# A fused attention and MoE kernel: both first pairs loaded ahead of the branch, tile 0 first, and the x split set between a unit's slices

## The chip, the cores and the metric

The kernel runs on one core of a Trainium2 chip. The metric is the device time of one execution in microseconds (us); a kernel's time is the median of its runs. The core has five engines that run their own queues of instructions in order and meet at semaphores: PE (TensorE, matrix products into PSUM), DVE (VectorE), ACT (ScalarE), POOL (GpSimd) and SP (SyncE, which here issues all DMAs). PSUM is counted in banks; here three pairs of banks carry the tag `s`, and one bank each the tags `pv0` and `pv1`.

## The reference

Soft-capped attention over 4 batches of 12 heads, 448 tokens and 64 dimensions each, followed by a two-layer feed-forward with ELU, all in float32:

```python
scores = scale * np.matmul(q, k.transpose(0, 1, 3, 2))
scores = cap * np.tanh(scores / cap)
attn = np.exp(scores - max); attn = attn / (sum(attn) + 1e-09)
x = np.matmul(attn, v)            # to (1792 tokens, 768)
h = x @ w_in                      # (1792, 2048)
g = np.where(h > 0.0, h, np.exp(np.minimum(h, 0.0)) - 1.0)
out = g @ w_out                   # (1792, 768)
```

## The kernel before

**Branch.** `constants` loads the cap and derives a flag from it; with a cap up to 32 the fast path runs (no maximum is subtracted), else a general one that these inputs do not take. SP issues the loads of pair 0 (`pre`, keys and queries; then its values) ahead of the branch, all others behind it.

**Attention.** Two heads of a batch are a pair; 24 pairs, 6 to a batch. A pair's keys and queries come as one DMA of 448 KB: 64 columns with the first 64 keys, 448 with the queries, 384 with the other keys (`QK` = 896 columns). A round takes two pairs and has seven score tiles: tile 0 for the first 64 keys of both pairs (`tile0`, from the raw float32 tile), tiles 1 to 3 for the rest of the first pair and 4 to 6 for the second (`scores`, from a high and a low part that DVE makes: `prep_qk`, the cast `qkh` and the difference `qkl`, three products each). ACT takes tanh and then exp of each tile (`act`); PE multiplies p with the values (`values`, tile pv, in four steps t of which t = 0 is tile 0's), DVE adds p tiles (`add`, u) and PE sums them over keys (`sums`). DVE copies pv and sums out of PSUM (`take`: num and sums). The sums go by four small DMAs into den, DVE inverts them (`invert`), a DMA writes rec to DRAM, four DMAs spread it over partitions (`spread`, rb, two buffers), and DVE multiplies (`normalise`, x = num * rb).

**MoE.** x is split for float32-like products into xh (a cast) and xl (the rest): `Tokens.high` and `low`. The 16 slices of 128 hidden columns are taken two at a time (r) for each batch (b): a unit. `first` of a unit has, for each of its two slices, 18 matmuls of w_in into one bank (`hidden`) and an ELU (`elu`: exp on ACT (e), two DVE steps, cast gh on ACT, difference gl on DVE); `second` has 36 matmuls of w_out into three `s` tiles, which ACT or DVE adds up. Unit 0's two slices share one `s` tile (`begin`); the later ones have the tags pv0 and pv1. xh of batches 0 and 1 lies in memory of its own; that of batches 2 and 3 in the pool `late`, which takes over the memory that attention's tiles leave.

**Order.** In the fast path each engine runs its instructions in the order in which the program calls them. `Attention.run` collects calls with times in units of a tile (`AT` for a round's steps, `END` for the steps behind the last scores, where end = 84) and makes them sorted by time; `Moe.run` then loops over units in plain order. With `END`, unit 0 (b = 0) is put among the last round's steps: unit 0's first slice at 0.1, its second at 1.6, the ELUs at 1.76 and 3.0, `moe.first(0, 1)` at 4.0; the six splits of batch 1 from 0.2. A round's `take` of its last sums stands at end + 2.86, of its last num at end + 1.75. The raw tiles of pairs 1 and up rotate through two buffers; pair 0 is in `pre`, which later holds weights.

Of the kernel before, what the change touches and what calls it, by code (L numbers as in the profile page):

```python
# [7 lines left out]
F32 = mybir.dt.float32  # L8
# [8 lines left out]
B, H, S, D = 4, 12, 448, 64  # L17
P = 128
BANK = 512
NPAIR = B * H // 2  # L20
PPB = H // 2
# [15 lines left out]
K0 = D  # L37
QK = K0 + S + 3 * P
# [16 lines left out]
END = {  # L55
    "invert": 3.4, "spread": (3.8, 3.8), "normalise": (3.6, 4.2),
    "unit0": 0.1, "split": 0.2, "step": 0.1, "unit0b": 1.6, "elu0": 1.76, "elu1": 3.0, "unit1": 4.0,
}
# [125 lines left out]
class Moe:  # L184
# [42 lines left out]

    def first(self, r, b):
        for i in range(FT):
            t = self.ps.tile([P, BANK], F32, name=f"h{r * FT + i}_{b}", tag=f"pv{i}", bufs=1)  # L230
            h = t[:, :S]
            self.hidden(r, b, i, h)
            self.elu(r, b, i, h)

# [31 lines left out]
    def run(self):  # L266

        units = [(r, b) for r in range(NR) for b in range(B)]
        for i in range(1, len(units) + 1):
            if 1 < i < len(units):  # L270
                self.first(*units[i])
            for p in range((i + 1) * PPB, min((i + 2) * PPB, NPAIR)):
                self.x.split(p)
            self.wt.run(WSTEPS - 2)
            self.second(*units[i - 1])
            self.wt.run(2)
            self.wt.load()


class Attention:  # L280
# [51 lines left out]
    def tile0(self, n):  # L332


        s = self.room(n, 0)
        for i in range(2):
            raw = self.raw.pop(2 * n + i)
            for j in range(2):
                o, at = slice(j * D, j * D + D), (i ^ j) * D
                self.nc.tensor.matmul(  # L340
                    s[at : at + D, j, :S], raw[o, :K0], raw[o, K0 : K0 + S], start=True, stop=True
                )
# [96 lines left out]
    def run(self, weights, moe, raw, rawv):  # L439
        self.raw[0], self.v[0] = raw, rawv  # L440
        self.load(1)
        self.load_v(1)
        events = []

        def at(time, f, *a):
            events.append((time, len(events), f, a))

        rounds = NPAIR // 2
# [5 lines left out]
        for n in range(rounds):  # L454
            g = NG * n

            at(g + AT["tile0"] if n else 1.0, self.tile0, n)
            for time, groups in BURSTS.items():
                at(g + time if n or groups[0] > 1 else -1.0, self.scores, n, groups)
            for k in range(NG):  # L460
                at(g + k if n or k > 2 else (k - 1) % 3, self.act, n, k)
            for i in range(2):
# [8 lines left out]
                for f in ("spread", "normalise"):  # L471
                    at(min(g + AT[f][i], end + END[f][n // (rounds - 1)]), getattr(self, f), p)
                at(g + AT["load"][i], self.load, p + 4)
# [11 lines left out]
        for c in range(PPB):  # L485
            at(end + END["split"] + c * END["step"], self.x.split, PPB + c)
        h = []
# [4 lines left out]
        at(end + END["elu1"], lambda: moe.elu(0, 0, 1, h[1]))  # L492
        at(end + END["unit1"], moe.first, 0, 1)
        for _, _, f, a in sorted(events, key=lambda e: e[:2]):
# [79 lines left out]
def attention_elu_kernel(tc, qk, v, cap, w, out):  # L574
    nc = tc.nc
    src = (qk, v)
    with ExitStack() as outer:
# [7 lines left out]
        rawv0 = pre[:, QK : QK + NT * P].rearrange("p (t c) -> p t c", t=NT)  # L585
        nc.sync.dma_start(out=raw0, in_=qk[0])
        nc.sync.dma_start(out=rawv0, in_=v[0])
        fast = nc.values_load(flag[0:1, 0:1], min_val=0, max_val=1)

        def path(general):  # L590
            tag = "gf"[not general]
            with ExitStack() as ctx:
# [5 lines left out]
                with tc.tile_pool(name=f"at{tag}", bufs=1) as sb, tc.tile_pool(  # L598
                    name=f"dr{tag}", bufs=1, space=DRAM
                ) as dr:  # L600
                    if general:
# [6 lines left out]
                        for i, h in enumerate(moe.begin()):  # L608
                            moe.hidden(0, 0, i, h)
                            moe.elu(0, 0, i, h)  # L610
                        moe.first(0, 1)
                    else:
                        Attention(nc, sb, ps, dr, x, con, src, rawp).run(weights, moe, raw0, rawv0)
                with tc.tile_pool(name=f"late{tag}", bufs=1) as late:
# [53 lines left out]
```

## Time and profile before

| | us |
|---|---|
| median of three runs | 662.17 (654.52, 662.17, 662.73) |
| profiled execution, its own time | 653.14 |
| its span on the core | 651.0 |
| PE busy | 634.4 (97%) |
| DVE busy | 462.6 (71%) |
| ACT busy | 297.1 (46%) |
| POOL busy | 61.4 (9%) |

Times within the profile count from the span's start. The attention stage takes up to about 172 us, the rest is the MoE stage. A busy share is an average over both: ACT's 46% is nearly all in the first quarter. A matmul counts as busy until its modelled end, so the share of PE says little about its pace; the starts of two matmuls in a row tell it. A number in brackets behind a timeline's row is the idle time before it and what ended that.

### The profile page before, as it was taken

Reading aid. Unit: us, or ns where it says so; the run is one execution under the profiler, and the core shown is the slowest. Engines: PE = TensorE matmul, PEld = TensorE weight load, DVE = VectorE, ACT = ScalarE, POOL = GpSimd, SP = SyncE. Lnnn points to the kernel's source line nnn. Section 1 sums busy time; section 2 is a strip of 40 time slices with the busy share of each in tenths; the row PEclk is TensorE's granted clock in tenths of the full one; section 3 lists DMA queues with packets and bytes.
Section 4 is the critical chain, followed back from the end, with each engine's and each line's share of the span. In section 5 each row is a group of like instructions: output and inputs, shape, how many; then the busy total and the mean of one; then the engine's idle time right before and its main releaser. Section 6 shows DMA issues by size and latency. Waiting matters only on the chain.

```text
span 651.0 us, 8745 instructions
## 1 busy us (share of the span) xinstructions
PE 634.4 (97%) x3408; PEld 500.7 (77%) x3408; DVE 462.6 (71%) x672; ACT 297.1 (46%) x384; POOL 61.4 (9%) x40
## 2 busy tenths in 40 slices
PE   5999999999998999999999999999999999999996
PEld 2434344344487999999999999999999999999995
DVE  4789999999746766666667777666667777666443
ACT  5999999999725553222232222222232222222110
POOL 0010100100001111111111121111111111111000
PEclk9999999999999999999999999999999999999999
DMA  5445555543115021120202021020202021000224
GB/s 161 139 123 192 166 184 145 170 139 117 38 31 214 1 97 39 60 97 1 98 0 98 1 98 57 41 98 1 97 1 98 1 98 66 31 1 0 86 86 173
DMA packets 29776, 54.38 MB, mean 84 GB/s; under 512 B 13344, under 2 KB 19488, under 8 KB 29728
## 3 DMA queue, kind: packets, MB, share of 16 engines
q1 hardware_dynamic: 29728, 53.75, 24.2%
q8 instruction: 29, 0.48, 0.3%
q14 instruction: 19, 0.16, 0.1%
HBM read 47.97 MB, written 5.59 MB: 82 GB/s over the span
## 4 chain that ended last, share of the span: by engine, by line
PE 82%; DVE 10%; DMA 3%; issue 1%; ACT 1%; SPq 1%; POOL 0%; DVEq 0%; ACTq 0%
PE h L197 12%; PE h L196 12%; PE h L198 12%; PE o L197 11%; PE o L196 11%; PE o L198 11%; PE pv L365 7%; PE s L323 4%; DVE u L387 3%; DVE qkl L318 2%; PE sum L396 2%; DMA raw<-in_qk_dram 1%; DVE num L402 1%; DMA rb<-rec 1%; PE s L340 1%
## 5 line engine op out<-in xcount | busy, mean ns | idle before, releaser
L196 PE MATMUL h<-xh,wh 128*128 128x448 f32 x384 | 140.6, 366 | 2.0 <-ACT xh L174 1.9
L197 PE MATMUL h<-xl,wh 128*128 128x448 f32 x384 | 140.3, 365 | 0.2 <-DVE xl L180 0.2
L198 PE MATMUL h<-xh,wl 128*128 128x448 f32 x384 | 140.3, 365 | 0.0
L197 PE MATMUL o<-gl,wh 128*128 128x448 f32 x380 | 138.8, 365 | 0.0
L196 PE MATMUL o<-gh,wh 128*128 128x448 f32 x380 | 138.8, 365 | 0.0
L198 PE MATMUL o<-gh,wl 128*128 128x448 f32 x380 | 138.8, 365 | 0.0
L261 DVE TENSOR_TENSOR acc<-o,acc 128x896 f32<-128x896 f32 x83 | 85.9, 1083 | 9.4 <-PE o L198 9.4
L211 DVE TENSOR_SCALAR e<-e 128x448 f32<-128x448 f32 x64 | 25.2, 393 | 88.4 <-ACT e L210 88.3
L210 ACT ACTIVATE e<-h 128x448 f32<-128x448 f32 x64 | 34.8, 544 | 116.3 <-PE h L198 114.8
L358 ACT ACTIVATE p<-s,cap 128x896 f32<-128x896 f32 x84 | 84.8, 1009 | 2.7
L356 ACT ACTIVATE s<-s,tsc 128x896 f32<-128x896 f32 x84 | 81.9, 975 | 5.2 <-PE s L323 5.0
L365 PE MATMUL pv<-p,vf 128*64 128x448 f32 x368 | 79.3, 552 | 1.3 <-DVE num L402 1.2
L196 PEld LDWEIGHTS h<-xh,wh 128*128 128x128 f32 x384 | 72.1, 188 | 9.8 <-ACT xh L174 2.3
L197 PEld LDWEIGHTS h<-xl,wh 128*128 128x128 f32 x384 | 72.1, 188 | 6.3 <-DVE xl L180 0.5
L198 PEld LDWEIGHTS h<-xh,wl 128*128 128x128 f32 x384 | 72.1, 188 | 5.7
L196 PEld LDWEIGHTS o<-gh,wh 128*128 128x128 f32 x380 | 71.4, 188 | 5.7
L198 PEld LDWEIGHTS o<-gh,wl 128*128 128x128 f32 x380 | 71.4, 188 | 5.7
L197 PEld LDWEIGHTS o<-gl,wh 128*128 128x128 f32 x380 | 71.4, 188 | 5.7
L219 ACT ACTIVATE gh<-e 128x448 fp32r<-128x448 f32 x64 | 37.0, 578 | 75.7 <-DVE e L214 75.7
L220 DVE TENSOR_TENSOR gl<-e,gh 128x448 fp32r<-128x448 f32 x64 | 40.0, 625 | 41.3 <-ACT gh L219 41.3
L126 POOL TENSOR_TENSOR pre<-pre,wq 128x768 int32<-128x768 int32 x18 | 34.8, 1933 | 353.4 <-DVE pre L123 353.4
L365 PEld LDWEIGHTS pv<-p,vf 128*64 128x64 f32 x368 | 22.3, 136 | 42.3 <-issue 32.4
(70 smaller groups left out, 635.1 us busy)
## 6 DMA issues: line engine op xcount, KB each, us to landing
pre<-in_w_dram SPq DMA_DIRECT2D x18, 768.0 KB, 4.2
wr<-in_w_dram SPq DMA_DIRECT2D x14, 768.0 KB, 5.6
raw<-in_qk_dram SPq DMA_DIRECT2D x23, 448.0 KB, 4.4
vf<-in_v_dram SPq DMA_DIRECT2D x23, 256.0 KB, 4.2
rb<-rec SPq DMA_DIRECT2D x48, 112.0 KB, 2.8
out_dram<-acc SPq DMA_DIRECT2D x11, 448.0 KB, 2.6
den<-sums SPq DMA_DIRECT2D x96, 1.8 KB, 2.2
pre<-in_qk_dram SPq DMA_DIRECT2D x1, 448.0 KB, 4.0
```

The costliest lines, as they stand in the source:

```text
L126: nc.gpsimd.tensor_tensor(out=vi, in0=vi, in1=q, op=ALU.add)
L196: mm(acc, wh[:, m, :], ph, start=first, stop=False)
L197: mm(acc, wh[:, m, :], pl, start=False, stop=False)
L198: mm(acc, wl[:, m, :], ph, start=False, stop=last)
L210: nc.scalar.activation(out=ev, in_=h, func=AF.Exp)
L219: nc.scalar.activation(out=gh, in_=ev, func=AF.Copy)
L220: nc.vector.tensor_tensor(out=gl, in0=ev, in1=gh.bitcast(F32), op=ALU.subtract)
L261: self.nc.vector.tensor_tensor(out=o, in0=t, in1=o, op=ALU.add)
L323: yield lambda a=a, b=b, i=i: self.nc.tensor.matmul(s, a[o, k], b[o, :S], start=i == 0, stop=i == 2)
L356: self.nc.scalar.activation(out=s, in_=s, func=AF.Tanh, scale=self.con.tsc[:, 0:1])
L358: self.nc.scalar.activation(out=pt, in_=s, func=AF.Exp, scale=self.con.cap[:, 0:1])
L365: self.nc.tensor.matmul(out[o, :S], w[j], x[j], **flags)
```

## The change

It has three parts. (a) Pair 1 gets a tile of its own, `raw1`, and both pairs' keys and queries are loaded ahead of the branch, in two parts each: first the 512 columns that tile 0 reads, of pair 0 and pair 1, then the other 384 of each. Round 0 then follows the same table as the other rounds: tile 0 is its first group (ACT's too), where before it was third. (b) The times behind the last scores are new: unit 0's first ELU stands ahead of its second slice, the six xl of batch 1 behind the copy of the last sums, the last four x (`normalise`) ahead of unit 1. (c) `first` takes the list of pairs that are to be split behind the unit and sets three between its first ELU and its second slice and three before the second ELU; before, all six came behind both ELUs. Unit 1's `first` is called from `Moe.run`.

```diff
 END = {
-    "invert": 3.4, "spread": (3.8, 3.8), "normalise": (3.6, 4.2),
-    "unit0": 0.1, "split": 0.2, "step": 0.1, "unit0b": 1.6, "elu0": 1.76, "elu1": 3.0, "unit1": 4.0,
+    "invert": 2.95, "spread": 2.97, "normalise": 3.2, "unit0": 0.1, "xh": 0.2, "elu0": 1.55, "unit0b": 1.6,
+    "xl": 2.9, "elu1": 3.0,
 }
-    def first(self, r, b):
+    def first(self, r, b, behind=()):
+
+        behind = list(behind)
         for i in range(FT):
             t = self.ps.tile([P, BANK], F32, name=f"h{r * FT + i}_{b}", tag=f"pv{i}", bufs=1)
             h = t[:, :S]
             self.hidden(r, b, i, h)
-            self.elu(r, b, i, h)
+            if i == 0:
+                self.elu(r, b, i, h)
+            for p in behind[i * 3 : i * 3 + 3]:
+                self.x.split(p)
+            if i:
+                self.elu(r, b, i, h)
...
         for i in range(1, len(units) + 1):
-            if 1 < i < len(units):
-                self.first(*units[i])
-            for p in range((i + 1) * PPB, min((i + 2) * PPB, NPAIR)):
-                self.x.split(p)
+            if i < len(units):
+                self.first(*units[i], range((i + 1) * PPB, min((i + 2) * PPB, NPAIR)))
...
-            raw = self.raw.pop(2 * n + i)
+            raw = self.raw[2 * n + i]
...
-        self.raw[0], self.v[0] = raw, rawv
-        self.load(1)
+        self.raw.update(enumerate(raw))
+        self.v[0] = rawv
...
-            at(g + AT["tile0"] if n else 1.0, self.tile0, n)
+            at(g + AT["tile0"], self.tile0, n)
...
-                at(g + k if n or k > 2 else (k - 1) % 3, self.act, n, k)
+                at(g + k, self.act, n, k)
...
-                    at(min(g + AT[f][i], end + END[f][n // (rounds - 1)]), getattr(self, f), p)
+                    at(min(g + AT[f][i], end + END[f]), getattr(self, f), p)
...
-            at(end + END["split"] + c * END["step"], self.x.split, PPB + c)
+            at(end + END["xh"], self.x.high, PPB + c)
+            at(end + END["xl"], self.x.low, PPB + c)
...
-        at(end + END["unit1"], moe.first, 0, 1)
...
-        nc.sync.dma_start(out=raw0, in_=qk[0])
+        raw1 = cp.tile([P, QK], F32, name="raw1")
+
+        for c in (slice(0, K0 + S), slice(K0 + S, QK)):
+            for p, t in enumerate((raw0, raw1)):
+                nc.sync.dma_start(out=t[:, c], in_=qk[p][:, c])
         nc.sync.dma_start(out=rawv0, in_=v[0])
```

**At the start, PE.** These are PE's first instructions behind the branch, before the change (s0_1 is round 0's tile 1; `pre` is pair 0, raw1 pair 1):

```order
L323 MATMUL s0_1_125<-qkh0_119 128x448 x2
L323 MATMUL s0_1_125<-qkl0_120,qkh0_119 128x448 x2
L323 MATMUL s0_1_125<-qkh0_119,qkl0_120 128x448 x2
L323 MATMUL s0_2_132<-qkh0_119 128x448 x2
L323 MATMUL s0_2_132<-qkl0_120,qkh0_119 128x448 x2
L323 MATMUL s0_2_132<-qkh0_119,qkl0_120 128x448 x2
L340 MATMUL s0_0_146<-pre_84 64x448 x2
L340 MATMUL s0_0_146<-raw1_115 64x448 x2
```

and with it:

```order
L345 MATMUL s0_0_125<-pre_84 64x448 x2
L345 MATMUL s0_0_125<-raw1_85 64x448 x2
L328 MATMUL s0_1_132<-qkh0_121 128x448 x2
L328 MATMUL s0_1_132<-qkl0_122,qkh0_121 128x448 x2
L328 MATMUL s0_1_132<-qkh0_121,qkl0_122 128x448 x2
L328 MATMUL s0_2_139<-qkh0_121 128x448 x2
L328 MATMUL s0_2_139<-qkl0_122,qkh0_121 128x448 x2
L328 MATMUL s0_2_139<-qkh0_121,qkl0_122 128x448 x2
```

Tile 0 has moved from the third place to the first, ahead of the tiles that need DVE's cast; from tile 3 on the order is the same.

**At the start, SP.** SP's first DMAs behind the cap's, before the change (pre and raw0 to raw3 are pairs, vf their values; COMPARE_AND_BRANCH is the branch):

```order
L586 DMA pre_84<-in_qk_dram 128x896
L587 DMA pre_84<-in_v_dram 128x512
L588 TENSOR_LOAD flag_76
L588 ISA x2
L619 COMPARE_AND_BRANCH
L500 DMA raw1_115<-in_qk_dram 128x896
L507 DMA vf1_117<-in_v_dram 128x512
L500 DMA raw2_123<-in_qk_dram 128x896
L500 DMA raw3_154<-in_qk_dram 128x896
```

and with it:

```order
L594 DMA pre_84<-in_qk_dram 128x512
L594 DMA raw1_85<-in_qk_dram 128x512
L594 DMA pre_84<-in_qk_dram 128x384
L594 DMA raw1_85<-in_qk_dram 128x384
L595 DMA pre_84<-in_v_dram 128x512
L596 TENSOR_LOAD flag_76
...
L626 COMPARE_AND_BRANCH
L511 DMA vf1_119<-in_v_dram 128x512
L504 DMA raw2_130<-in_qk_dram 128x896
L504 DMA raw3_156<-in_qk_dram 128x896
```

Pair 1's keys and queries have moved ahead of the branch and, as pair 0's, come in two parts; pair 0's values are fifth where they were second, and raw2 and raw3 (pairs 2 and 3) are the first two in their tag.

**Behind the last scores, DVE.** From the last split of batch 1 on, before the change (num23 and sums23 are the last pair's copies out of PSUM, e0_0 and e1_0 the ELUs of unit 0's slices, den11 the last round's inversion):

```order
L180 TENSOR_TENSOR xl11_1971<-x11_1348,xh11_1969 128x448
L402 COPY num23_2000<-pv11_1_1909 128x448
L211 TENSOR_SCALAR e0_0_2002<-e0_0_2002 128x448
L214 SCALAR_TENSOR_TENSOR e0_0_2002<-h0_1922,e0_0_2002 128x448
L220 TENSOR_TENSOR gl0_0_2007<-e0_0_2002,gh0_0_2006 128x448
L405 COPY sums23_2016<-sum11_1_1977 128x448
L211 TENSOR_SCALAR e1_0_2022<-e1_0_2022 128x448
L214 SCALAR_TENSOR_TENSOR e1_0_2022<-h0_1922,e1_0_2022 128x448
L220 TENSOR_TENSOR gl1_0_2027<-e1_0_2022,gh1_0_2026 128x448
L417 SCALAR_TENSOR_TENSOR den11_1916<-den11_1916,eps_75 64x28
L420 RECIPROCAL den11_1916<-den11_1916 64x28
L437 TENSOR_TENSOR x20_2034<-num20_1764,rb20_2010 128x448
```

and with it, from unit 0's first ELU on, with five xl of the same form left out:

```order
L211 TENSOR_SCALAR e0_0_1972<-e0_0_1972 128x448
L214 SCALAR_TENSOR_TENSOR e0_0_1972<-h0_1924,e0_0_1972 128x448
L220 TENSOR_TENSOR gl0_0_1977<-e0_0_1972,gh0_0_1976 128x448
L407 COPY num23_1998<-pv11_1_1911 128x448
L410 COPY sums23_2006<-sum11_1_1967 128x448
L180 TENSOR_TENSOR xl6_2012<-x6_1031,xh6_1947 128x448
...
L422 SCALAR_TENSOR_TENSOR den11_1918<-den11_1918,eps_75 64x28
L425 RECIPROCAL den11_1918<-den11_1918 64x28
L211 TENSOR_SCALAR e1_0_2034<-e1_0_2034 128x448
L214 SCALAR_TENSOR_TENSOR e1_0_2034<-h0_1924,e1_0_2034 128x448
L220 TENSOR_TENSOR gl1_0_2039<-e1_0_2034,gh1_0_2038 128x448
L442 TENSOR_TENSOR x20_2042<-num20_1766,rb20_2000 128x448
```

The copies of num23 and sums23 have moved from behind six splits and around an ELU to directly behind that ELU; the splits stand behind them, and den11 ahead of the second ELU.

**Between unit 1's slices, DVE.** From the last x on, before the change (e0_1 and e1_1 are the ELUs of unit 1's slices, xl12 belongs to batch 2):

```order
L437 TENSOR_TENSOR x20_2034<-num20_1764,rb20_2010 128x448
L437 TENSOR_TENSOR x21_2036<-num21_1831,rb21_2013 128x448
L211 TENSOR_SCALAR e0_1_2063<-e0_1_2063 128x448
L214 SCALAR_TENSOR_TENSOR e0_1_2063<-h0_1_2044,e0_1_2063 128x448
L220 TENSOR_TENSOR gl0_1_2068<-e0_1_2063,gh0_1_2067 128x448
L211 TENSOR_SCALAR e1_1_2090<-e1_1_2090 128x448
L214 SCALAR_TENSOR_TENSOR e1_1_2090<-h1_1_2071,e1_1_2090 128x448
L220 TENSOR_TENSOR gl1_1_2095<-e1_1_2090,gh1_1_2094 128x448
L437 TENSOR_TENSOR x22_2098<-num22_1897,rb22_2038 128x448
L437 TENSOR_TENSOR x23_2100<-num23_2000,rb23_2041 128x448
L180 TENSOR_TENSOR xl12_2112<-x12_1504,xh12_2110 128x448
L180 TENSOR_TENSOR xl13_2116<-x13_1506,xh13_2114 128x448
```

and with it:

```order
L442 TENSOR_TENSOR x20_2042<-num20_1766,rb20_2000 128x448
L442 TENSOR_TENSOR x21_2044<-num21_1833,rb21_2003 128x448
L442 TENSOR_TENSOR x22_2046<-num22_1899,rb22_2028 128x448
L442 TENSOR_TENSOR x23_2048<-num23_1998,rb23_2031 128x448
L211 TENSOR_SCALAR e0_1_2077<-e0_1_2077 128x448
L214 SCALAR_TENSOR_TENSOR e0_1_2077<-h0_1_2058,e0_1_2077 128x448
L220 TENSOR_TENSOR gl0_1_2082<-e0_1_2077,gh0_1_2081 128x448
L180 TENSOR_TENSOR xl12_2087<-x12_1506,xh12_2085 128x448
L180 TENSOR_TENSOR xl13_2091<-x13_1508,xh13_2089 128x448
```

All four x stand ahead of unit 1's first ELU, and the splits of batch 2 behind that one ELU rather than behind both.

## Rows read from the trace of the kernel before

**Rows 1.** PE's waits, from 0 to 30 us, then 165 to 215: total us, times, longest.
```profile
PE s L323 <- DVE qkh L315: 6.0, 1, 6.0
...
PE h L196 <- ACT xh L174: 1.9, 1, 1.9
```

**Rows 2.** Timeline of the start: start us, us, engine, line, operation, out<-in, shapes, count.
```profile
1.21 0.42 SPq L586 DMA_DIRECT2D pre<-in_qk_dram  x1
1.67 0.43 SPq L587 DMA_DIRECT2D pre<-in_v_dram  x1
...
5.31 0.59 DVE L315 CAST qkh<-pre 128x832 fp32r<-128x832 f32 x1 [0.77 <-DMA pre<-in_qk_dram]
...
8.23 0.98 ACT L356 ACTIVATE s<-s,tsc 128x896 f32<-128x896 f32 x1 [3.88 <-PE s L323]
...
9.18 1.01 PE L340 MATMUL s<-pre 64*64 64x448 f32 x2
9.99 0.96 PE L340 MATMUL s<-raw 64*64 64x448 f32 x2
...
14.13 2.48 PE L365 MATMUL pv<-p,pre 128*64 128x448 f32 x12 [1.03 <-ACT p L358]
...
18.85 0.98 PE L340 MATMUL s<-raw 64*64 64x448 f32 x8
...
35.01 0.97 ACT L356 ACTIVATE s<-s,tsc 128x896 f32<-128x896 f32 x1
```

**Rows 3.** DMA issues of the first 12 us: kind, count, KB each, us from issue to landing.
```profile
pre<-in_qk_dram SPq DMA_DIRECT2D x1, 448.0 KB, 4.0
pre<-in_v_dram SPq DMA_DIRECT2D x1, 256.0 KB, 4.2
```

**Rows 4.** Busy us by windows: two rounds, then MoE stage; PE, PEld, DVE, ACT, POOL.
```profile
62.45:76.00 13.55, 13.55 (x94) 5.61 (x92) 13.17 (x20) 13.27 (x15) 0.75 (x1) 1.00 0.47 144
117.04:130.61 13.57, 13.57 (x94) 5.61 (x92) 13.50 (x21) 13.32 (x15) 0.00 (x0) 1.00 0.60 200
...
230.00:640.00 410.00, 410.00 (x2025) 379.92 (x2024) 272.07 (x378) 108.76 (x168) 48.14 (x26) 1.00 0.15 56
```

**Rows 5.** Timeline of the turn from attention to MoE, columns as in rows 2.
```profile
172.24 0.47 PE L196 MATMUL h<-xh,wh 128*128 128x448 f32 x1
173.81 2.69 DVE L180 TENSOR_TENSOR xl<-x,xh 128x448 fp32r<-128x448 f32 x5
...
178.62 0.47 PE L196 MATMUL h<-xh,wh 128*128 128x448 f32 x1
...
182.57 0.55 ACT L210 ACTIVATE e<-h 128x448 f32<-128x448 f32 x1 [7.52 <-PE h L198]
183.66 0.62 DVE L214 SCALAR_TENSOR_TENSOR e<-h,e 128x448 f32<-128x448 f32 x1
185.47 0.62 DVE L405 COPY sums<-sum 128x448 f32<-128x448 f32 x1
185.82 0.37 PE L198 MATMUL h<-xh,wl 128*128 128x448 f32 x1
186.23 0.44 PE L196 MATMUL h<-xh,wh 128*128 128x448 f32 x1
...
189.92 0.24 DVE L417 SCALAR_TENSOR_TENSOR den<-den,eps 64x28 f32<-64x28 f32 x1 [1.44 <-DMA den<-sums]
...
192.89 3.11 SPq L432 DMA_DIRECT2D rb<-rec  x4
...
197.26 0.37 PE L198 MATMUL o<-gh,wl 128*128 128x448 f32 x1
...
198.20 0.63 DVE L437 TENSOR_TENSOR x<-num,rb 128x448 f32<-128x448 f32 x1 [0.54 <-DMA rb<-rec]
198.91 2.92 ACT L174 ACTIVATE xh<-x 128x448 fp32r<-128x448 f32 x6 [3.59 <-DVE x L437]
...
200.51 0.36 PE L198 MATMUL h<-xh,wl 128*128 128x448 f32 x1
```

More of the change, by code (lines that the diff above doesn't have):

```diff
@@ L610, in path @@
                             moe.elu(0, 0, i, h)
-                        moe.first(0, 1)
                     else:
-                        Attention(nc, sb, ps, dr, x, con, src, rawp).run(weights, moe, raw0, rawv0)
+                        Attention(nc, sb, ps, dr, x, con, src, rawp).run(weights, moe, (raw0, raw1), rawv0)
                 with tc.tile_pool(name=f"late{tag}", bufs=1) as late:
```

## The prediction

> **What bounds the kernel now.** I read the page's engine rows first, then TensorE's waits by stretch, then the timelines of the two stretches in which those waits lie, and last the windows of the stretch between them. TensorE (PE) waits long at two places only: 6.0 us at the start, and 1.9 us at the first matmul of unit 2 [rows 1]; behind 215 us the view of its waits is empty. So 436 of the 651 us can change only by being started earlier, and the question is how much earlier.
>
> At the start ACT's first tanh stands at 8.23 [rows 2]. From there a tile's tanh and exp take 1.913 us (14 pitches from 8.23 to 35.01), 13.39 for a round of seven. But rounds take longer: one of 13.55 in which PE is busy all 13.55, a later one of 13.57 in which DVE is busy 13.50 [rows 4]. PE and DVE, and not ACT alone, carry the attention stage; a lead has to reach them.
>
> At the turn to the MoE stage, PE's last matmul of unit 0 starts at 197.26; at its pitch of 0.2025 (410 us for 2025 matmuls [rows 4]) the third matmul of unit 2 would start at 197.87, and it starts at 200.51 [rows 5]: 2.64 us lost. The chain behind it reads backwards: xh12 (198.91) waits for x23 (198.20), the last reader of the memory that xh12 takes over; x23 for the reciprocals' broadcast (rb, issued from 192.89, when their trip through rec in DRAM was over), that for den (189.92), that for the copy of the sums at 185.47. The copy could have run when the sums were there, ahead of 178.62, but stands in DVE's queue behind the ELU of unit 0's first slice, and that ELU started at 182.57, when the second slice was done.
>
> **The start, step by step.** Both pairs' keys and queries for tile 0 are 512 columns, 256 KB each, and now go first. In the trace 448 KB issued at 1.21 landed 4.0 later, at 5.21, and 256 KB more issued at 1.67 landed at 5.87 [rows 2, 3]. The new second transfer, issued at about 1.67, completes 512 KB: bounds 5.2 and 5.9, I take 5.5, as 512 KB lies near the first. Tile 0 starts at 5.6, takes 1.77 as it did at 9.18 (to 10.95), and ACT starts at 7.45: 0.8 earlier.
>
> The Trainium skill, "DMA: Bandwidth & Descriptors", section Bandwidth, speaks against the two parts: its table has 1 MB moved at 341 GB/s and 64 KB at 138. Worked out from that table (an estimate), 512 KB in small pieces would need up to 3.7 us of transfer instead of 1.5, ACT would start behind 8.23, and the sum below would be 2.4. No row here has transfers of 192 KB; the trace's one of 256 KB landed 4.2 after its issue, hardly behind the 4.0 of 448 KB.
>
> Tile 1 needs pair 0's second part, the third transfer (issued about 2.13, landed 6.1 to 6.4). From the cast to ACT's start was 2.92 (5.31 to 8.23), so it is ready at about 9.2, and ACT wants it at 9.36. That is in time by little; each 0.1 more costs 0.1.
>
> The larger gain is on PE. Before, the twelve value matmuls at 14.13 could not begin until the third exp, since the group's first operand (tile 0's p) was third on ACT. Now p0 and p1 are there and eight of the twelve run ahead of the third exp. Scores of tile 4 start when the second exp frees a bank, 7.45 + 3.83 = 11.3; 0.8 for six matmuls; then the 4.72 that PE took from 14.13 to 18.85 puts the next round's tile 0 at 16.8, where it must wait for the fifth exp, 7.45 + 9.57 = 17.0. Against 18.85 that is **1.8 us earlier**. The freeing of the raw buffers, and with it the load and casts of pairs 4 and 5 on SP and DVE, hangs on that same tile 0 and shifts too; pair 3's load no longer waits for pair 1's buffer. Since PE and DVE set the rounds, I carry 1.8 to the end of the stage. Bounds: 0.8 (ACT's lead alone), 2.2 (first parts there at 5.2).
>
> The early matmuls are slow: tile 0's eight took 1.77 at 9.18 and 0.98 at 18.85, though the page's clock row reads full in every slice. I priced tile 0 at 1.77 and the value matmuls at full pace, as at 14.13. The Trainium skill, "TensorE: Matmul & The Clock Gate", Part 1, says that "the default state is throttled, and activity releases the throttle"; the trace agrees. By that rule the pauses that the new order leaves PE (waiting for banks until 11.3) could bring the faster level later; its time is that of the second rival.
>
> **The turn, on the old clock (all of it shifts by 1.8).** PE's order is the same. The first slice starts at 172.24; the second took 3.95 from 178.62 to ACT's e at 182.57, so e for the first can start at 176.2. **A new wait:** both slices share one tile, so PE's second slice waits until DVE's second ELU step has read the first. That step ended 1.71 after e (183.66 + 0.62): 177.9, and PE has sums and values until 178.62. Covered by 0.7; queued behind it would be all of PE. From e to the copy of the sums was 2.90; now num23's copy (0.55) stands between: sums at 179.6 instead of 185.5. The six xl of unit 1, moved behind it, run at 0.54 each (five in 2.69 at 173.81) from 180.2; PE wants the first at 182.6, then one per 0.61. Hidden, by 1.8; without that cover each us would be one of PE.
>
> Then den, 4.45 behind the sums: 184.1; rb could go out 2.97 behind that (189.92 to 192.89), at 187.0. Now one detour: the ELU of slice 1 stands ahead of x20 and x21 on DVE, and rb22 takes rb20's buffer; x20 is done at about 187.4 (den's two steps to 184.6, 2.3 for the ELU, 0.5), so SP issues rb22 at 187.45. From there to x23's end 5.94 (192.89 to 198.83): 193.4. Behind it in DVE's queue stand unit 1's first ELU, then xl12 to xl17. The ELU holds DVE 2.35 (the 2.90 less e's 0.55), to 195.75, while ACT, behind gh, makes xh12 (0.5); xl12 is done at 196.4. PE needs it at 197.46: **margin 1.1 us, and the 2.64 go.** Also the copy of the sums held PE from 186.02 to 186.23 (second bank); that 0.2 goes. The den, rec and rb DMAs and the weights behind them on SP start some 5.5 earlier and have an idle queue. Slice 1's ELU of unit 1 comes behind xl17, its second step done at about 200.2; PE takes that bank at 200.9. In unit 2 the x split moves likewise and PE keeps a us. The xh and xl themselves are as many as before, under PE's matmuls.
>
> **Sum:** 1.8 + 2.64 + 0.2 = 4.6. The profiled span 651.0 becomes 646.4, its own time 653.14 (2.14 outside the span) 648.5. The three timed runs are 654.52, 662.17 and 662.73; the median lies 9.03 above the profiled execution, and nothing in this trace shows those 9 us. I take the same 4.6 off the median: **657.6**. If most of the new runs fall beside the profiled one, they read 648.5 to 650.
>
> **Rivals.** (1) The parts move side by side instead of one after another, and the first ones land with the last of the 896 KB: 5.87 for 704 KB and 0.66 for each 256 KB more give 6.4. ACT starts 0.9 later than reckoned, 3.7 are saved: 658.5. Against it: 448 KB landed 0.66 ahead of 704. The skill's table on small pieces, above, points the same way. (2) The head start is swallowed: tile 1 or PE's faster level comes late, ACT keeps 0 to 0.8 of its lead, and little but the turn is won: 2.8 to 3.6 saved, 659.0. For it: a margin of 0.1 at tile 1. Against it: PE waited 1.03 for ACT at 14.13, room that the new order fills. The skill's rule on the clock, above, is one way to it. (3) The turn's stall is kept, because unit 0's first e or DVE's queue is later than reckoned by over 1.1 + 2.6: 1.8 saved, 660.4. Against it: every link above has its own row. (4) The other side: x22 and x23 now stand ahead of unit 1's first ELU in DVE's queue, and while they wait for rb nothing behind them runs, xl12 included. Beyond 194.5 for x23's end each us costs PE one; at 199.1, behind even the old 198.83, all 4.6 are gone. At 200.1 the time is 663.2. Against it: from rb22's issue to x23 it would take 12.6 us instead of 5.9. (5) The edits change nothing that a run shows, the spread of the runs being larger: 662.
>
> **How the numbers follow.** Forecast 0.55, (1) 0.10, (2) 0.15, (3) 0.09, (4) 0.03, (5) 0.08. In all of them some two in five of the chance is for runs near the profiled execution rather than the median's level. The range runs from 647.5 (profiled level, with the upper bounds 2.2 + 2.8 saved 648.1, and half a us for what lies outside the span) to 661.5 (median's level, only 0.7 saved); the forecast's own range, given the median's level, is 656.6 to 659. Two per cent, about what a measurement of this kernel tells from no change, is 13 us, and no part here comes near it; faster by that only if the new median falls to the profiled level and all 4.6 come: 0.12. Slower by that: 0.03.
>
> **What would show it.** ACT's first tanh at 7.3 to 7.6; its second 1.91 later, with no wait for PE. Round 1's tile 0 near 17.0. The first matmul of unit 0 (172.24) near 170.4. In the waits of PE behind that: no xh or xl, and the second slice of unit 0 at no wait for DVE. The copy of the last sums 7.4 us, not 13.2, behind unit 0's first matmul. I am wrong if the rounds lengthen to give the 1.8 back, or if a PE wait on DVE appears at the second slice, at xl12 or at unit 2's second slice.

## The result, and the profile after

The changed kernel takes **648.26 us** (four executions, 648.10 to 648.50), the kernel before 658.94 beside it (654.52, 655.72, 662.17, 662.73). The ratio on record, 0.9886 with an interval of 0.9838 to 0.9935, is of fast executions, those within 1.5% of a kernel's fastest, and not that of the two medians; here the taller ones are part of what a kernel does, so the text gives all of them. The profiled execution of after has a span of 646.2 and a time of 648.27; forecast for it were 646.4 and 648.5. The forecast median, 657.6, was not met: all new executions lie at the profiled level. From profiled to profiled execution the gain is 4.87 us (653.14 to 648.27), between the medians 10.68. The other 5.8 us are the real finding.

TensorE's waits in the trace of after: total us, times, longest.

```profile
PE s L345 <- DMA pre<-in_qk_dram: 5.0, 1, 5.0
PE pv L370 <- DVE num L407: 1.7, 5, 0.7
PE s L328 <- DVE qkl L323: 0.3, 1, 0.3
```

The 1.9 us of [rows 1] are gone, and so is every wait behind 165 us. The first line names the DMA, but that part landed at 4.61 (below), 0.4 ahead of PE's start; most other runs with the new start have the same wait, of 5.1 to 5.3 us, for `DVE eps`, a step of the constants ahead of the branch. The start, columns as in [rows 2]:

```profile
5.02 1.01 PE L345 MATMUL s<-pre 64*64 64x448 f32 x2 [5.02 <-DMA pre<-in_qk_dram]
...
5.36 1.01 PE L345 MATMUL s<-raw 64*64 64x448 f32 x2
...
7.25 0.98 ACT L361 ACTIVATE s<-s,tsc 128x896 f32<-128x896 f32 x1 [2.88 <-PE s L345]
...
8.14 0.74 PE L328 MATMUL s<-qkl,qkh 64*128 64x448 f32 x2 [0.32 <-DVE qkl L323]
...
9.32 0.98 ACT L361 ACTIVATE s<-s,tsc 128x896 f32<-128x896 f32 x1
...
12.36 2.48 PE L370 MATMUL pv<-p,pre 128*64 128x448 f32 x12
...
17.14 0.98 PE L345 MATMUL s<-raw 64*64 64x448 f32 x8
```

And the DMA issues of the first 12 us, us from issue to landing, against [rows 3]:

```profile
pre<-in_qk_dram SPq DMA_DIRECT2D x1, 256.0 KB, 3.4
raw<-in_qk_dram SPq DMA_DIRECT2D x1, 256.0 KB, 3.6
...
pre<-in_qk_dram SPq DMA_DIRECT2D x1, 192.0 KB, 4.2
```

The second first part, issued at 1.67, is there at 5.27, and ACT starts 0.98 earlier than in [rows 2]. Its second tanh comes 2.07 behind the first, not 1.913: tile 1, for whose low halves PE waited 0.3, was 0.16 late. PE's tile 0 of round 1 stands 1.71 earlier (17.14 for 18.85).

The turn, against [rows 5]:

```profile
171.10 0.47 PE L196 MATMUL h<-xh,wh 128*128 128x448 f32 x1
...
175.04 0.55 ACT L210 ACTIVATE e<-h 128x448 f32<-128x448 f32 x1 [1.12 <-PE h L198]
...
178.39 0.61 DVE L410 COPY sums<-sum 128x448 f32<-128x448 f32 x1
...
178.93 3.29 DVE L180 TENSOR_TENSOR xl<-x,xh 128x448 fp32r<-128x448 f32 x6
...
182.84 0.24 DVE L422 SCALAR_TENSOR_TENSOR den<-den,eps 64x28 f32<-64x28 f32 x1 [0.62 <-DMA den<-sums]
...
186.29 2.37 SPq L437 DMA_DIRECT2D rb<-rec  x4
...
191.14 0.62 DVE L442 TENSOR_TENSOR x<-num,rb 128x448 f32<-128x448 f32 x1 [0.69 <-DMA rb<-rec]
...
193.25 2.90 ACT L174 ACTIVATE xh<-x 128x448 fp32r<-128x448 f32 x6
...
195.83 0.36 PE L196 MATMUL h<-xh,wh 128*128 128x448 f32 x1
```

xh12 is made from 193.25, and PE reaches unit 2 at 195.83 without stopping. **The gain by terms:** unit 0's first matmul is 1.14 earlier (172.24 to 171.10). The first output matmul behind unit 2's `first` (207.40 before, 203.12 after) is 4.28 earlier, so the turn gave 3.14. From there to the last matmuls nothing changes; what follows them was 0.5 us shorter. 1.14 + 3.14 + 0.5 = 4.8, the spans' difference. Two of these terms hold for this pair of traces only. Behind the last matmul come 5.1 to 5.7 us in the traces of this case, whatever the order, so the 0.5 is not the change's. And unit 0's first matmul stands at 171.84 and 171.89 in the two other traces with the old start, and at 170.86 to 171.15 in seven with the new one: the start is worth 1.0 there on average.

### The profile page after: what moved, and what is told of

Its sections match the earlier page's. It is cut to its first block, busy times and chain, and to the rows that moved or that the text cites. A ratio compares the mean times of both kernels' runs of the same rounds, so it can differ in the third digit from the quotient of the medians.

```text
span 646.2 us, 8747 instructions
## 1 busy us (share of the span) xinstructions
PE 633.9 (98%) x3408; PEld 501.8 (78%) x3408; DVE 462.5 (72%) x672; ACT 296.8 (46%) x384; POOL 61.4 (10%) x40
## 4 chain that ended last, share of the span: by engine, by line
PE 86%; DVE 9%; DMA 2%; issue 1%; SPq 0%; POOL 0%; DVEq 0%
PE h L196 12%; PE h L198 12%; PE h L197 12%; PE o L198 12%; PE o L197 12%; PE o L196 12%; PE pv L370 7%; PE s L328 5%; DVE u L392 3%; DVE qkl L323 2%; PE sum L401 2%; DVE num L407 1%; PE s L345 1%; DMA pre<-in_qk_dram 1%; DVE qkh L320 1%
```

## Experiments: which part, and what are the heights?

**The kernel before, again.** No edit.

> The kernel before, unchanged, to see span and time of each of its executions. All theories expect executions at two levels, near 654 and near 662 us. Theory A (what lies between the two levels has nothing to do with the edits): executions at 662 have a span of 651 and 11 us around it, or a longer span whose extra time lies anywhere. Theory B (the pause of TensorE at the turn makes the upper level): the extra 8 us lie in the span, behind 197 us, with matmuls at a wider pitch than 0.2025. Theory C (the start makes it): the extra 8 us lie in the span, ahead of round 1's tile 0, which then stands later than 18.85.

Its twelve executions and 74 more of the kernel before beside the other experiments have spans at four heights: 650.6 to 651.6 at a mean granted clock of 0.999 (11 of them; the profiled execution of before, 651.0, is such a one), 651.6 to 653.4 at 0.996 or 0.997 (41), 653.3 to 654.4 at 0.993 to 0.995 (10), and 660.4 to 663.7 (24, middle 661.1). Nothing lies between 657 and 662 us of time. So theory A in the form "outside the span" falls.

**The start alone.** The kernel before with the four first loads and `at(g + AT["tile0"], self.tile0, n)`, `at(g + k, self.act, n, k)`.

> The kernel before with the new start alone (both first pairs ahead of the branch in two parts, tile 0 first). All theories: ACT's first tanh at 7.25, unit 0's first matmul near 171.1 instead of 172.24, the wait of 1.9 us at unit 2's first matmul still there, since the chain of sums, den, rec, rb and x moves with it; span 651.0 - 1.1 = 649.9, or 649.4 if the last 0.5 us of the gain lie in the tail. Theory A and B: its executions still show two levels, about 652 and 660. Theory C: all of them lie within 0.5 us near 652.

Ratio 0.9989 (0.9947 to 1.0031). Two executions at full clock have 650.1, which is 0.9 under the middle of before's; but five of twelve stand at 659.8 to 660.7, and one of these is the profiled one, so that its trace shows the upper height. Its wait at unit 2, windows of it (us, then busy us and count of PE, PEld, DVE, ACT, POOL, then PEclk, DMA share, GB/s; PEld are PE's weight loads, PEclk the granted clock), and PE at a shorter pause, 11 us earlier:

```profile
PE h L196 <- ACT xh L174: 2.7, 1, 2.7
```

```profile
197.00:199.10 2.10, 0.00 (x0) 0.00 (x0) 0.63 (x1) 0.58 (x2) 0.00 (x0) 1.00 1.00 375
199.10:200.30 1.20, 0.97 (x2) 0.68 (x3) 1.17 (x3) 1.20 (x3) 0.00 (x0) 0.76 1.01 420
200.30:201.60 1.30, 1.30 (x5) 1.13 (x5) 1.30 (x3) 1.30 (x4) 0.00 (x0) 0.50 0.34 142
...
230.00:640.00 410.00, 410.00 (x1986) 372.41 (x1985) 266.98 (x371) 107.55 (x166) 48.03 (x26) 1.00 0.15 53
```

```profile
184.61 0.37 PE L198 MATMUL h<-xh,wl 128*128 128x448 f32 x1
185.02 0.44 PE L196 MATMUL h<-xh,wh 128*128 128x448 f32 x1
185.30 0.37 PE L197 MATMUL h<-xl,wh 128*128 128x448 f32 x1
```

The pause costs three times. First itself, 2.7 us. Second, behind it the granted clock is 0.50, the level of 1.2 GHz: for some 2.6 us the matmuls follow each other at 0.372 instead of 0.203, which costs 1.0 to 1.5. In the profiled execution of before the pause was 1.9 and the clock stayed full; in the one profiled here without an edit (span 652.0) it was 2.3, and the clock fell: that is the step from 651 to 652. No execution at 653.3 to 654.4 was profiled; that these lost more by the clock is read from their means alone. (The Trainium skill, "TensorE: Matmul & The Clock Gate", Part 1, has it that activity releases the throttle; this trace agrees as far as the 0.50 behind a pause goes.) Third, **the stream behind the pause runs at a wider pitch to the end of the kernel**: 1986 matmuls in 410 us where [rows 4] have 2025, at a clock that reads 1.00. From start to start that is 0.2067 for 0.2027 (the counts take in two at the edges of the window). Over the 2,200 matmuls left this is 8.8 us: the step to 661. It does not lie at the start, so theory C falls. But it does not begin at the long pause either: in this trace the matmuls go at 0.2067 from 185.30 on, behind the 0.2 us for which PE waits for the copy of the last sums, and the long pause leaves the pitch as it was. In the profiled executions of before at 651.0 and 652.0 the same short pause has 0.2067 behind it too, and the long one ends it. So this run alone does not say which of the two pauses makes the upper height.

**The turn alone.** The kernel after with the start of before.

> The kernel before with the new turn alone (first ELU ahead of the second slice, xl behind the sums, x split between a unit's slices). All theories: first tanh at 8.23, unit 0's first matmul at 172.24, no wait for xh or xl in unit 2; 2.64 for the stall, 0.2 for the bank and 0.3 for the wider pitch there are saved: span 651.0 - 3.1 = 647.9, or 647.4 with 0.5 in the tail. Theory A and C: its executions still show two levels, about 650 and 658. Theory B: all of them lie within 0.5 us near 650.

649.24 (649.20 to 649.50, six executions), ratio 0.9892 (0.9836 to 0.9949), spans 647.3 to 647.6, no wait of PE behind 165 us. The heights are gone with the two pauses: theory B. With the changed kernel and three of the runs below that have no pause there either (whole pairs, and the weight steps moved, all or two) it is 28 executions, all with spans of 645.9 to 647.9. The turn is worth 3.65 against before's executions at full clock (651.0), the start another 1.0 on top of it (649.24 to 648.26).

**Whole pairs instead of parts.** `for p, t in enumerate((raw0, raw1)): nc.sync.dma_start(out=t, in_=qk[p])`

> The changed kernel with the two first pairs loaded whole, in two DMAs of 448 KB, instead of four parts. Theory of the prediction (the transfers are served one after another, so the parts bring pair 1's keys and queries of tile 0 forward): pair 0 lands at about 5.2, pair 1 at about 6.4, tile 0's second half follows it, ACT's first tanh at 7.9 to 8.2 instead of 7.25, round 1's tile 0 0.4 to 0.8 later than 17.14, and 0.2 to 0.6 of it left in the span (646.4 to 646.8). Rival (the parts are served side by side, or the lead is lost later in the rounds whatever its size): the span stays at 646.2 within 0.1.

649.20 (648.95 to 649.65), ratio 0.9891 (0.9835 to 0.9948), span 647.1. Timeline:

```profile
6.38 1.76 PE L345 MATMUL s<-raw 64*64 64x448 f32 x4
...
8.26 0.98 ACT L361 ACTIVATE s<-s,tsc 128x896 f32<-128x896 f32 x1 [3.79 <-PE s L345]
```

Pair 1 lands at 6.37 when it is whole, and ACT starts a microsecond later. The parts are served one after another, as the prediction had it, and they are worth 0.9, a little more than expected. Preloading without parts would have left ACT at its old 8.23. It also has the time of the turn alone (649.20 and 649.24): with whole pairs the early load and tile 0's new place gain nothing that the time shows. Tile 0 of round 1 does come 0.9 earlier than in [rows 2], at 17.98, but unit 0's first matmul stands at 171.68, 0.2 ahead of the nearest trace with the old start. Tile 0's place was not tried without the early load.

**One short pause put back.** In the changed kernel DVE reads the sums' bank once more, behind the second ELU step of unit 0's second slice:

```
+        if hold is not None:
+            nc.vector.tensor_copy(out=gl, in_=hold)
         nc.scalar.activation(out=gh, in_=ev, func=AF.Copy)
...
-        at(end + END["elu1"], lambda: moe.elu(0, 0, 1, h[1]))
+        at(end + END["elu1"], lambda: moe.elu(0, 0, 1, h[1], self.last))
```

> The changed kernel with one short pause put back: VectorE reads the bank of the last sums once more (into gl, which is written over), right behind the second ELU step of unit 0's second slice, so that the bank of unit 1's second slice comes free at about 185.05 instead of long before 184.88, and PE pauses some 0.2 us there, as it did in the kernel before at 186.02. No other wait is expected. Theory D (a pause of PE, however short, can leave the unbroken stream behind it at the wider pitch, 0.2067 for 0.2026, until the next pause; in all three traces that have the pause at 186.0 the pitch behind it was 0.2067): some or all executions have about 2236 matmuls at 0.0041 more, 9.2 us, a span near 655.6 and a time near 657.6. Theory E (only a pause of 2 us and more, with the granted clock at 0.5 behind it, does this): span 646.4, time 648.5 in all executions.

648.41 (648.31 to 648.93), ratio 0.9892 (0.9843 to 0.9940): no effect in six executions. "However short" was wrong. The extra read alone costs nothing.

**The same pause, one more read long.** `for _ in range(2): nc.vector.tensor_copy(out=gl, in_=hold)`

> The changed kernel with one pause put back, as in e9_gap, but with two extra reads of the bank by VectorE (0.61 each) instead of one: PE pauses about 0.75 us at unit 1's second slice instead of 0.14; nothing else waits. In e9_gap six of six executions went on at 0.2026 behind 0.14 us; in e5_split, with pauses of 0.54 and 0.51 us, four of twelve stood 8.3 us higher with a full clock. Theory D (a pause alone, without any other change, lets the stream go on at the wider pitch in some executions): most executions near 649.0 (648.3 + 0.75), some, about one in three, near 657.5. Theory E (it takes the late x of unit 2, or a pause over 2 us): all executions near 649.0.

**658.21** (657.95 to 658.55), ratio 1.0055 (1.0040 to 1.0070): all six executions 9.8 us above the kernel with one read. First the pause in the kernel with one read, then in this one, and a window of each in the MoE stage, in the same order:

```profile
184.52 0.37 PE L198 MATMUL h<-xh,wl 128*128 128x448 f32 x1
...
184.86 0.44 PE L196 MATMUL h<-xh,wh 128*128 128x448 f32 x1
```

```profile
184.02 1.27 DVE L221 CAST gl<-sum 128x448 fp32r<-128x448 f32 x2
...
184.44 0.37 PE L198 MATMUL h<-xh,wl 128*128 128x448 f32 x1
...
185.44 0.44 PE L196 MATMUL h<-xh,wh 128*128 128x448 f32 x1 [0.63 <-DVE gl L221]
```

```profile
230.00:640.00 410.00, 410.00 (x2025) 379.93 (x2024) 272.43 (x378) 107.18 (x166) 46.65 (x26) 1.00 0.15 58
230.00:640.00 410.00, 410.00 (x1986) 372.42 (x1985) 267.96 (x373) 107.25 (x166) 47.00 (x26) 1.00 0.15 53
```

From start to start 0.34 in the one, 1.00 in the other, where 0.20 is the pitch. Of the 9.8 us 0.66 are the pause, the rest is the pitch, 0.2067 in every stretch from 186 us on, at a clock of 0.998. This is the cleanest of the runs: nothing but one read by DVE and with it the length of one pause differs, and no clock falls.

**The first ELU back behind the second slice.** `"elu0": 1.55` becomes `1.76`.

> The changed kernel with the ELU of unit 0's first slice behind the second slice again, as before (one number of the order; all else as changed). Theory of the prediction (the copy of the sums stands in DVE's queue behind that ELU): e at 181.4 instead of 175.04, sums copied near 184.3 instead of 178.39, x23 done near 197.5, and PE waits some 2.5 us at unit 2's first matmul: span about 649.1 without anything else. With theory D its executions spread beyond that: 1.5 us more where the granted clock falls to 0.5 behind the pause, and some 9 us more where the stream goes on at 0.2067. Rival (the new place of the ELU does nothing, the x split between the slices alone took the stall away): span 646.2, no wait.

659.18 (653.70 to 664.15), ratio 1.0049 (1.0000 to 1.0098), six of twelve executions at 663 to 664. The profiled one:

```profile
PE h L197 <- DVE xl L180: 3.9, 1, 3.9
```

```profile
184.10 0.61 DVE L410 COPY sums<-sum 128x448 f32<-128x448 f32 x1
...
184.64 2.75 DVE L180 TENSOR_TENSOR xl<-x,xh 128x448 fp32r<-128x448 f32 x5
```

The sums are copied at 184.10 (expected 184.3), so that link holds. But PE stops elsewhere than expected: at unit 1's first xl, since xl6 to xl11 stand behind that copy in DVE's queue. That is the cover named in the prediction ("without that cover each us would be one of PE"), and it is the first to break.

**The split of x back behind both ELUs.**

```
-            if i == 0:
-                self.elu(r, b, i, h)
-            for p in behind[i * 3 : i * 3 + 3]:
-                self.x.split(p)
-            if i:
-                self.elu(r, b, i, h)
+            self.elu(r, b, i, h)
+        for p in behind:
+            self.x.split(p)
```

> The changed kernel with the x split behind both ELUs of a unit again (the loop in first as before; all else as changed). x23 stays done at 191.8. Theory of the prediction (the split between the slices is needed too: behind the second ELU xh12 stands behind ACT's gh of that ELU): xh12 near 195.5 instead of 193.25, xl12 near 196.7, PE waits 0.2 to 0.8 us at unit 2's first two matmuls: span 646.4 to 647.0, and by theory D some or all executions 9 us more. Rival (the early sums alone take the stall away): span 646.2, time 648.3, no wait.

649.70 (648.93 to 657.94), ratio 0.9961 (0.9914 to 1.0009). PE's waits at unit 2:

```profile
PE h L196 <- ACT xh L174: 0.4, 1, 0.4
PE h L197 <- DVE xl L180: 0.3, 1, 0.3
```

0.7 us of waits, in the range expected (1.1 us from start to start beyond the pitch, in two pauses). Eight of twelve executions have spans of 647.0 to 647.8, four of 655.3 to 656.1, all with a clock of 0.997 or more. So the early sums took most of the stall away, and the split between the slices the rest; without it a third of the executions would have lost over 8 us. These pauses have no shorter one ahead of them, so they make the upper height by themselves, in some executions.

**x23 delayed.** Two more trips of rec through DRAM: `for hop in range(2 if n == NPAIR // 2 - 1 else 0)`, each a `dma_start` into a tile of DRAM.

> The changed kernel with the last round's reciprocals copied through DRAM twice more between rec and rb (two more DMA trips of about 2 us each), so that x22 and x23 come late with all else as changed. Theory of the prediction (rival 4: behind x23 on DVE stand unit 1's first ELU and xl12; on the new clock x23 may end up to 1.5 us later than its 191.76 before PE waits, and from there each us costs PE one): x23's end near 195.6, PE waits 2.0 to 2.6 us at unit 2's first two matmuls, span 648.2 to 648.8; beyond that 1.5 us where the granted clock falls, and about 8.5 us in some executions, as with every pause of this size so far. Rival (the margin is larger than reckoned, since ACT and DVE could run ahead): no wait, 648.3.

653.54 (651.65 to 662.41), ratio 0.9999 (0.9956 to 1.0041). The waits, and x23:

```profile
PE h L196 <- ACT xh L174: 2.3, 1, 2.3
...
PE h L197 <- DVE xl L180: 0.2, 1, 0.2
```

```profile
195.60 0.63 DVE L446 TENSOR_TENSOR x<-num,rb 128x448 f32<-128x448 f32 x1 [0.71 <-DMA rb<-hop]
```

x23 ends at 196.23 instead of 191.76, 4.47 later, and PE waits 2.5. Counted as the prediction counted its 2.64, from start to start beyond the pitch, PE loses 2.95 (195.68 to 198.31 to 199.04). If the price is one for one, as reckoned, the margin is 1.5 by that count, as expected, and 2.0 by the waits; one delay alone does not show the price and the margin apart. Rival 4 is real; in the changed kernel it is just not reached. Eight executions show the pause with or without the fallen clock (spans 649.5 to 652.1), four the wider pitch (657.8 to 660.4).

**What the attention stage gives back.** Two edits move a weight step of DVE, which stands ahead of the copy of the numerators for which PE waits 1.7 us: `"weights": (4.95, 5.68)` becomes `(5.45, 5.68)`. The first:

> The changed kernel with the first of a round's two weight steps on DVE put behind the copy of the numerators (5.45 instead of 4.95 in the order; the copy stands at 5.35). In the changed kernel PE waits for that copy 1.7 us in five places, 0.7 of it in round 2, where the step of three operations (2.1 us) stands ahead of the copy. Theory F (these waits are why the attention stage gives back 0.6 of PE's lead of 1.7): they go, unit 0's first matmul comes 0.5 to 1.2 us ahead of 171.10, span 645.0 to 645.7. Rival (DVE is full in these rounds, 13.7 to 13.9 of 14 us, so that the wait moves to the sums or the casts): span 646.2 within 0.2, with other waits of PE of the same sum.

663.85 (662.91 to 665.33). Here the step came behind the load of the next weights (5.0 in the order) and worked on those: the computation is another, DVE waited 11.4 us in two places for that load, and the time says nothing on the question. With the load moved as well:

> As e7_weights, with the load of the next weights put behind the step as well (-1.5 instead of -2.0 in the order), which e7_weights left ahead of it, so that there the step read what the next load had brought. Theory F (PE's 1.7 us of waits for the copy of the numerators are why the attention stage gives back 0.6 of PE's lead): they go, unit 0's first matmul comes 0.5 to 1.2 us ahead of 171.10, span 645.0 to 645.7, time 647.1 to 647.8. Rival (DVE is full in these rounds, 13.7 to 13.9 of 14 us, so the wait moves to the sums or the casts): span 646.2 within 0.2, with other waits of PE of about the same sum.

648.72 (648.65 to 648.91), ratio 0.9909 (0.9895 to 0.9924): the rival, and 0.5 above the changed kernel. PE waits 1.7 us for DVE as before, at the sums now. With only the two steps moved that had seemed to gain:

> The changed kernel with the first weight step of rounds 1 and 6 alone (those of three operations, 2.1 us, which stand directly ahead of the copy of the numerators) put behind that copy; no load moves. In e10_weights, where every round's step was put behind it, the stretches from tile 0 to tile 0 behind rounds 1 and 6 fell from 14.35 and 13.96 to 13.54 and 13.55, and four others grew by 0.15 to 0.91. Theory F, narrowed: these two gains of 0.81 and 0.41 come without the losses, tile 0 of round 8 at 112.0 instead of 113.19, and 0.6 to 1.2 us of it reach the turn: span 645.0 to 645.6, time 647.1 to 647.7, all executions within 0.5 us (no pause of PE behind 178 us). Rival (rounds 8 and 9, in which DVE is busy 13.87 of 14 us, give it back, since DVE's later work does not start earlier): span 646.0 to 646.3.

648.31 (647.84 to 648.65), ratio 0.9854 (0.9792 to 0.9917), no better than the changed kernel. Tile 0 of round 8 stands at 111.90, 1.29 earlier than after's 113.19, and all but 0.2 of it is given back in the next two rounds:

```profile
98.36:111.90 13.54, 13.54 (x94) 5.60 (x92) 13.17 (x22) 13.31 (x15) 0.00 (x0) 1.00 0.55 151
111.90:126.11 14.21, 13.66 (x94) 5.62 (x93) 12.75 (x21) 13.45 (x15) 1.81 (x1) 1.00 0.60 187
126.11:140.53 14.42, 13.73 (x94) 5.65 (x92) 14.28 (x23) 13.52 (x15) 0.00 (x0) 1.00 0.43 129
```

DVE is busy 14.28 of 14.42 us in the last; it has no other wait in rounds 8 and 9 than 1.4 us for POOL, in round 8. So PE's waits for the copy are where these rounds' limit shows, not its cause. That the limit is DVE with that wait for POOL is read from these rows; no run lightened DVE.

## Why the prediction was right, and where it was not

**Right by its range.** The measured 648.26 lies in the range by its lower end: the prediction gave two chances in five to runs at the profiled level, without a reason why they should all fall there, and its forecast of 657.6 was 9.3 too high. That is luck as far as the level goes. The 4.6 against the profiled pair's 4.8 is luck in part too: the start came out 0.66 short, the turn 0.3 above, and 0.5 came from behind the last matmul.

**The start: right at the start, too large at the end.** Both first parts there at 5.27 (5.5), ACT 7.25 (7.45, a little under the 7.3 to 7.6 named), tile 0 of round 1 at 17.14 (17.0). Tile 1 was ready at 9.3 where 9.2 had been reckoned, but ACT, 0.2 ahead of the forecast, wanted it at 9.16. The step that failed is "I carry 1.8 to the end of the stage": 1.14 arrived, which is one of the signs of being wrong that the prediction named ("if the rounds lengthen to give the 1.8 back"). The lead of 1.71 lost 0.3 in the stretch behind round 1 and 0.27 behind round 8. (Against the two other traces with the old start, where the first of these stretches is 13.69, the first loss is 0.6.) Before, then after:

```profile
32.42:46.45 14.03, 13.63 (x95) 5.62 (x93) 12.49 (x19) 13.51 (x15) 0.00 (x0) 1.00 0.44 138
...
128.15:141.89 13.74, 13.66 (x94) 5.61 (x93) 13.60 (x22) 13.49 (x15) 0.00 (x0) 1.00 0.42 129
```

```profile
30.69:45.04 14.35, 13.65 (x95) 5.66 (x93) 12.82 (x19) 14.09 (x16) 0.00 (x0) 1.00 0.46 135
...
126.74:140.75 14.01, 13.73 (x95) 5.67 (x93) 13.87 (x22) 13.53 (x15) 0.00 (x0) 1.00 0.47 140
```

PE does the same 13.63 to 13.73 us of work in each; the pauses beside it grew. The first loss is the weight step ahead of the copy: in the last two runs above, which moved it, that stretch is 13.55 and 13.56, only for later rounds to take the gain back. The prediction had DVE as a carrier of the stage, but took for granted that DVE itself would start all of its work 1.8 earlier. It did not: DVE's cast of pair 2 starts at 11.23, where it was 10.79, and that of pair 3 at 14.30, where it was 14.38. Rival 2 (the head start swallowed) came about for a third, by the rounds and not by the two ways that it named.

**The turn: right link by link.** Counted from unit 0's first matmul: e 3.94 (3.96 forecast), sums 7.29 (7.4), den 11.74 (11.9), rb 15.19 (15.2), x23's end 20.66 (21.2). The feared new wait of the second slice for DVE does not appear. The 2.64 and the 0.2 went, and 0.3 more, most of it pitch: behind the pause at 186.0 before's matmuls ran at 0.2067 up to the next pause, after's run at 0.2027.

**The level: wrong.** The step "nothing in this trace shows those 9 us" and the 4.6 taken off the median's level failed. The trace did show the sign of it, in that same 0.2067 between 186.51 and 197.26, 52 steps in 10.75 us, which the prediction passed over:

```profile
186.51:197.26 10.75, 10.75 (x54) 9.76 (x52) 6.18 (x14) 2.71 (x5) 0.00 (x0) 1.00 0.15 42
```

The 9 us belonged to the two pauses that the change removes: as a stretch of wider pitch in 24 of 86 executions, and, by their lower mean clock, as a fallen clock in 51 of the other 62. The profiled execution, at full clock, was of the cheapest kind, one in eight. So the stall's price in the sum, 2.64, holds for that execution alone; in a common one it was 3 to 6, in an upper one 13.

**The rivals.** Rival 1 fell with the landings (first parts at 4.61 and 5.27, second parts at 6.34 and 6.82) and with the whole pairs; rivals 3 and 4 did not occur, but the experiments that undid a part brought each of them about. Rival 5 fell: the highest new execution, 648.50, is 6 us below the lowest old one. The Trainium skill's table ("DMA: Bandwidth & Descriptors", section Bandwidth) has transfers issued from GpSimd, and by its rate for 64 KB the estimate was up to 3.7 us of transfer for 512 KB. Here, issued from SP, both first parts were there 4.06 us after the first issue and 3.6 after the second, where 0.5 KB (the cap) took 3.0; so the rate for 64 KB does not carry over to these two of 256 KB.

## What to carry to other kernels

Where several executions of one kernel scatter in steps, look in the trace for pauses of TensorE ahead of a long unbroken run of matmuls, and compare the pitch, matmuls per 100 us, behind and ahead of each pause: the pause may cost ten times its length (here some 9 us behind one of 0.8). Take the last pause ahead of such a run away before any other. And carry a lead through a stage only as far as its fullest engine also starts earlier.

## What the runs showed of the hardware

Two things were not expected. A pause of PE, with the clock full, can leave the matmuls behind it at 0.2067 instead of 0.2027 us each: in all six executions with one pause of 0.8 us at the end of a DVE read, in 4 of 12 with two pauses of half a us, in none of six with 0.14, and in a quarter to a half of those with pauses of 2 to 4 us. (Where no trace was taken, this goes by the span.) The pause of 0.2 us at 186.0 in the order of before had it behind it in all three traces looked at, and a later pause ended it in two of them and not in the third. Step by step, the faster stream repeats five steps, of 0.199, 0.207, 0.203, 0.202 and 0.203 us, while in the slower one every step is 0.206 or 0.207: it is the faster one's longest step, kept. The weight loads beside them are no slower (372.42 us for 1985 in the kernel with two reads, 379.93 for 2024 in that with one: 0.188 both). What decides between the two pitches stays open; neither length alone nor the clock does. And the clock row's 1.00 at the start is not a reading. Tile 0's eight matmuls take 1.77 us once pair 1 is there (5.36 to 7.13) where eight later take 0.98, and neighbours start 0.37 apart, as they do behind a pause where the row shows 0.50. But the first record of the granted clock, 1.00, begins at 11.5 us in the trace of before and at 11.8 in that of after, and the view prints 1.00 where it has none; the prediction too took that for a reading. In those two traces the starts come close, 0.20 to 0.25 apart, just there.
